# Forgetting attention and a SwiGLU block on one core: the first stage's loads in another order, with memsets that hold the loads of the next batches

## The chip, the cores and the metric

The kernel runs on one core of a Trainium2 chip. The metric is the device time of one execution in microseconds (us), from the start of the program to its end on the chip; the time of a kernel is the median of several executions. The engines are called PE (TensorE, matrix products), ACT (ScalarE), DVE (VectorE), POOL (GpSimd) and SP (SyncE, which here only issues transfers). DMA transfers are issued by SP and ACT into one hardware queue (q1 in the profile) and by POOL into a software queue (q0).

## What is computed

Eight batches of eight heads, 576 tokens, 64 features per head. First a causal attention whose scores carry a decay from a gate f, then a SwiGLU block over all 4608 tokens. Inputs and output are float32.

```python
# q, k, v: (8, 8, 576, 64); f: (8, 8, 576)
scores = q @ k.transpose(0, 1, 3, 2) / sqrt(64)
cum = cumsum(log(clip(f, 1e-4, 1.0)), axis=-1)
scores = where(causal, -1e9, scores + cum[:, :, :, None] - cum[:, :, None, :])
attn = softmax(scores, axis=-1)
x = (attn @ v).transpose(0, 2, 1, 3).reshape(4608, 512)

g, val = x @ w_gate, x @ w_val        # (512 x 1536) each
out = (g * sigmoid(g) * val) @ w_out  # (1536 x 512)
```

## The kernel before

**A plan made at build time.** The class `Plan` (L33) is a list scheduler in Python. Every step of the kernel is an `op` (L52) with an engine or several engines and their costs, the steps that it comes `after`, the buffers that it takes or uses, a priority `key` (the smallest runnable key goes first on its engine), a due time `ready`, and for a transfer its length `dma` and its weight `pkt`. `run` (L76) plays this model forward, and where it starts a step it emits the step's instructions. What reaches the chip is only the order of the instructions on each engine, the choice of buffers, and semaphores for the dependences of data; the due times and costs leave no other mark. In the model, transfers share the DMA between the rings of SP, ACT and POOL in proportion to `pkt` (L111 and L126, with a factor 1.2 where more than one ring is busy), and a transfer counts as landed 1.0 us after its last byte. While the plan has PE idle between 0.6 us and `IDLE_TO` (L904), it emits filler matmuls that nothing reads (`dummy`, L892; `idle=` in L896).

**The work.** A pair is two heads of one batch: 32 pairs, four per batch. For each pair the scores (`score`, L655) are computed transposed, keys on the partitions, from the buffer QK, whose rows hold 64 features and four rows of decay; ACT takes the exponential (`expo`, L663), POOL sets the upper triangle to zero (`mask`, L672), PE multiplies with the values in VB (`weigh`, L686; a column of ones gives the sums), DVE inverts the sums (`invert`, L693) and scales (L700 or L702), PE transposes the result (`flip`, L710), and `put` (L715) writes it to xT. The feed-forward block takes tiles of tokens from xT: twelve groups each of matmuls with wg and wv (`gate`, L787), the activation from tanh on ACT (L791) and two DVE steps (L795, L799), then per 128 tokens twelve matmuls with wo (`project`, L803), a copy (L808) and a store by SP (L811). The first tile is batch 0's 256 first tokens and the second its 320 others, which share their buffers; then come eight tiles of 512 tokens.

**The first stage, batch 0.** q and k are loaded in two halves, a (256 tokens, `ld_a`, L484) and b (320 tokens, `ld_b`, L487), for four heads each, then cast (`cast_1`, L490, through L334 on ACT or L336 on DVE), transposed by PE (L509) and copied to QK (`straighten1`). v goes straight to VB, cast by POOL's transfers (`ld_vc`, L550), in five chunks of 128 tokens (the last of 64). Attention is done for the first half of the tokens of all four pairs and then for the second half.

**The first stage, batch 1** (`FIRST = 2` batches come this way). q and k of a pair are loaded by SP (`ld_qk`, L481), cast on POOL or DVE (`cast_t`, L493), transposed (L498), copied. Its decay rows are four transfers (`row`, L437, in the list `o_row1`) from `dec`, which `blank` (L367 to L371) and `up`, `high`, `rest`, `middle` and `low` (L421 to L434) have filled. v comes as in batch 0. Four buffers BF, into which `cast_t` writes, are blanked by POOL (L363).

**Batches 2 to 7.** POOL casts q and k of a pair into an array `qk_d` in DRAM (`narrow`, L520), SP loads them transposed (`turned`, L529), then the decay rows from `dec_d` (`rows`, L532), which two transfers `dec_out` (L467) wrote earlier. v is loaded by SP into natv (`ld_v`, L539) and cast on POOL (L336). A pair may start these steps at `release(p)` (L478): `PACE0 + (p - 8) * PACE`.

**Weights.** wg, wv and wo come in three chunks each, cast by POOL's transfers (`weights`, L783 and L780).

**What sets the order around the change.** The constants at the end (L900 to L909) are due times and limits of the plan: `W_AT` and `WO_AT` for the chunks of the weights, `Q1_AT` for the pairs of batch 1, `V1_AT` for its v, `DEC_AT` for the decay steps; `FK` is the key of the shared first two tiles of the feed-forward block (`ffn`, L823), `HOLD` holds the first transposes, and `SF` and `TF` end the time in which scores, and transposes of batch 1, may use other PSUM banks. The keys are given in the list at L859 to L890, of which the change touches these:

```python
    for n in range(2):
        values(0, n, -6 + 0.1 * n)
    for n in range(2, NB):
        values(0, n, 2 + 0.1 * n)
```

So two chunks of batch 0's v go first on POOL's queue (key -6), then the first chunks of wg and wv (-5.5), then the other three chunks of v (2).

Of the kernel before, what the change touches and what calls it, by code (L numbers as in the profile page):

```python
# [32 lines left out]
class Plan:  # L33


    PIPE = {"PE": 0.25, "ACT": 0.2, "DVE": 0.2, "POOL": 0.2}

    SPAN, WARM = 3.413, 0.40

# [9 lines left out]
        w = int(t / self.SPAN)  # L49
        self.done_work[w] = self.done_work.get(w, 0.0) + dur * share  # L50

    def op(self, eng, fn, after=(), take=(), use=(), key=0.0, ready=0.0, dma=None, pkt=50.0):  # L52
        o = Op(eng, fn, list(after), list(take), list(use), key, ready, dma)
        o.pkt = pkt
        for b in o.use:
            b.left += 1
        self.ops.append(o)
        return o
# [17 lines left out]
    def run(self, idle=None):  # L76
# [7 lines left out]
        ready = {e: [] for e in engines}  # L84
# [17 lines left out]
        while left:  # L102
# [4 lines left out]
            while events and events[0][0] <= t + 1e-9:  # L107
                _, _, kind, o = heapq.heappop(events)
                if kind in ("queue", "dma"):
                    busy_rings = [r for r in rings.values() if r]  # L110
                    whole = sum(r[0][1].pkt for r in busy_rings) / (1.2 if len(busy_rings) > 1 else 1.0)  # L111
                    for r in busy_rings:
                        r[0][0] -= (t - moved) * r[0][1].pkt / whole
                        while r and r[0][0] < 1e-6:
                            over, n = r.pop(0)
                            if r:
                                r[0][0] += over
                            n.done = t + 1.0
                            push(n.done, "end", n)
                            push(n.done, "done", (n, None, False))  # L120
                    moved = t
                    if kind == "queue":
                        rings[o.ran].append([o.dma, o])
                    busy_rings = [r for r in rings.values() if r]
                    if busy_rings:
                        whole = sum(r[0][1].pkt for r in busy_rings) / (1.2 if len(busy_rings) > 1 else 1.0)  # L126
# [85 lines left out]
PADS = (512, 960, 1344)  # L212
NQK, NPT0, NPT, NVB, NNV, NXN, NTH, NHH, NOT, NRC = 8, 6, 5, 3, 6, 3, 4, 16, 3, 4
FIRST = 2
LEAD = 12.0
PACE, PACE0 = 9.83, 60.3


@with_exitstack
def kernel(ctx, tc, q, k, v, f, w_gate, w_val, w_out, out):  # L220
# [213 lines left out]
        nc.vector.tensor_sub(dec[3][:, 1], r1, dec[2][:, 1])  # L434

    def row(e, r, b, a, z):
        E[e].dma_start(  # L437
            out=QK[D + r : D + r + 1, b * FB : (b + 1) * FB, :, a:z].rearrange("o p x s -> o (p x) s"),
            in_=dec[r][b * H : (b + 1) * H, :, a:z],
        )  # L440
# [19 lines left out]
    m = op(("DVE", dve(n, False)), middle, after=[x], key=k0, tag="middle")  # L460
    x = op(("DVE", dve(n, False)), low, after=[m], key=k0, tag="low")
    gates = [u, g, m, x] + turned_cum
    o_row1 = [op(("SP", SPi), row, r, 1, 0, S, after=gates + o_dec, key=95, dma=0.9, pkt=60.0, tag=("row1", r)) for r in range(4)]
    o_warm = op(("ACT", 1.4), lambda e: nc.scalar.activation(warm, cum[:1, :1], AF.Exp), after=lns + prior, key=-4)

    def dec_out(e, i):
# [75 lines left out]
        m = min(P, S - n * P)  # L542
        copy(e, VB[hvb[b].i][:m, n, :, :D], natv[bv.i][:m])

    v_ready = {}
    LOADK = {0: 0, 1: 300}

    def ld_vc(e, b, n):
# [2 lines left out]

    def values(b, n, key, after=(), ready=0.0):
        if b < FIRST:
            v_ready[b, n] = op(("POOL", 0.9), ld_vc, b, n, after=[v_ready[b, 0]] if n and b else [], key=key, ready=ready, dma=1.5 if n < NB - 1 else 0.8, pkt=25.0,
                               **({"take": [hvb[b]]} if n == 0 else {"use": [hvb[b]]}), tag=("v", n))
            return
        bv = Buf("nv")
        o = op(("SP", SPi), ld_v, b, n, bv, take=[bv], key=key, dma=1.6 if n < NB - 1 else 0.8, pkt=25.0, after=after,
               ready=ready)
        eng = ("POOL", pool(H * D))  # L560
        v_ready[b, n] = op(
            eng, cast_v, b, n, bv, after=[o, o_vb[b % NVB]], use=[bv], key=key,
            **({"take": [hvb[b]]} if n == 0 else {}),
        )
        if n:
            v_ready[b, n].use.append(hvb[b])
            hvb[b].left += 1
            v_ready[b, n].after.append(v_ready[b, 0])
# [5 lines left out]
    def first_queries(g, key_a, key_b):  # L574
        for part, kk0, ld, m, nt, lo in (("a", key_a, ld_a, P, TA, 0), ("b", key_b, ld_b, PB, TB, HALF)):
            n = 4 * nt * D
            casts = []
            for x, nm in enumerate("qk"):
                kk = kk0 + 0.1 * x + 0.2 * g
                bn = Buf("nata") if part == "a" else Buf("natb", "natw")  # L580
                o1 = op(("ACT", 0.55) if part == "a" and x and g else ("SP", SPi), ld, g, nm, bn, take=[bn], key=kk, ready=2.0 if part == "a" and x and g else 0.0,
                        dma=1.06 if part == "a" else 1.2, pkt=33.0 if part == "a" else 60.0, tag=("ld" + part, g, x))
                o2 = op({"DVE": n / 1350 + 0.12, "ACT": act(n)}, cast_1,
                        lambda bn=bn, part=part: nat["nata"][bn.i] if part == "a" else nat[bn.pool][bn.i][:PB], part, x, g, m,
                        after=[o1, o_one[part]], use=[bn], key=kk, tag=("cast" + part, g, x))
# [2 lines left out]
            for h4 in range(4):  # L588
# [5 lines left out]
                first_turned.append(o3)  # L594
                first = p not in took
                o4 = op({"ACT": act(2 * m * nt) + 0.05, "DVE": dve(2 * m * nt)}, straighten1, h, bt, m, nt, lo,
                        after=[o3] + ([took[p]] if not first else []),
                        take=[hqk[p]] if first else [], use=[bt] if first else [bt, hqk[p]], key=kk, tag=("str" + part, h))
# [4 lines left out]
    def queries(p, key, after=(), ready=0.0):  # L603
        done = []
        b = p // FB
        if b < FIRST:
            rest = []
            for x, nm in enumerate("qk"):
                bn, bb, bt = Buf("nat", ("natb", 60.0)), Buf("bf"), Buf("t", ("f", TF), ("s", 22.0))
                kk = key + 2 * x  # L610
                o1 = op(("SP", SPi), ld_qk, p, nm, bn, take=[bn], key=kk, dma=1.2, pkt=100.0, after=after, ready=ready + 0.9 * x,
                        tag=("ldqk", p))
                o2 = op({"POOL": 1.05, "DVE": 0.7}, cast_t,
                        lambda bn=bn: nat[bn.pool if bn.pool == "nat" else "natb1"][bn.i], bb,
                        after=[o1] + o_bf, take=[bb], use=[bn], key=kk, tag=("cast", p))
                o3 = op(("PE", mm(*[P] * QT)), turn, bb, bt, after=[o2, o_id], take=[bt], use=[bb], key=kk, tag=("turn", p))
                for u in range(2):
                    first = not rest
                    rest.append(op(
                        {"ACT": 0.65, "DVE": 0.75}, straighten, p, x, u, bt,  # L620
                        after=[o3] + ([rest[0]] if rest else []),
                        take=[hqk[p]] if first else [], use=[bt] if first else [bt, hqk[p]], key=kk, tag=("str", p),
                    ))
            done = rest
        else:
            ns = [op(("POOL", 0.55), narrow, p, x, key=key + x, ready=release(p) - LEAD, dma=0.9, pkt=60.0, after=after, tag=("narrow", p))
                  for x in range(2)]
            ts = []
            for j in range(2):
# [231 lines left out]
    for n in range(2):  # L861
        values(0, n, -6 + 0.1 * n)
    for n in range(2, NB):
        values(0, n, 2 + 0.1 * n)
    for c in range(NCH):
        for nm, t, src in (("g", wg, w_gate), ("v", wv, w_val)):
            w_ready[nm, c] = op(("POOL", SW), weights, t, src, c, key=-5.5 if not c else 20 + 4 * c, dma=3.0, pkt=95.0,
                                ready=W_AT[c], tag=("w", nm, c))
    for c in range(NCH):
        w_ready["o", c] = op(("POOL", SW), weights, wo, w_out, c, after=wo_free, key=30 + c, dma=3.0, pkt=95.0, ready=WO_AT[c],  # L870
                             tag=("w", "o", c))
    for p in range(FB, FIRST * FB):
        queries(p, 100 + 10 * p, ready=Q1_AT[p - FB])
# [35 lines left out]
TF = 21.3  # L909


# [28 lines left out]
```

## Time and profile before

| what | value |
|---|---|
| runs | 405.73, 406.21, 403.23 us; median 405.73 |
| profiled execution, its time | 407.84 us |
| its span | 406.1 us |
| mean granted clock of PE | 0.976 |
| PE busy | 389.8 us (96%), 3141 matmuls |
| DVE, ACT, POOL busy | 222.8, 219.8, 148.3 us |
| moved by DMA | 50.05 MB; q1 36.25 MB, q0 12.98 MB |
| matmuls L787 (wg, wv), L803 | 111.6 + 111.0, 105.1 us |
| matmuls L655, L686 | 74.8, 44.0 us |

The span is the stretch from the first to the last recorded instruction of the profiled execution, and all starts in the traces count from its beginning. The granted clock is the share of full speed that the throttle gave to PE. Busy times are sums over an engine's instructions; the engines run beside each other, so only what PE, or whatever ends last, waits for is on the path. "L787" is line 787 of the kernel.

### The profile page before, as it was taken

How to read it: one execution, taken by the hardware profiler on the slowest of the kernel's cores; microseconds unless marked ns; L12 is line 12 of the kernel's file. 1: busy time of each engine (PE TensorE's matmuls, PEld its weight loads, DVE VectorE, ACT ScalarE, POOL GpSimd, SP SyncE). 2: the span in 40 equal slices, each digit the busy share in tenths (PEclk: the TensorE clock that was granted, in tenths of full speed). 3: DMA queues.
4: the chain of work that ended last, by engine and by line, in shares of the span. 5: the costliest groups of instructions: out<-in, count | busy, mean ns of one | idle time of the engine just before them, and what ended most of it. 6: DMA issues, size and time to landing. Idle time of an engine off the chain costs nothing.

```text
span 406.1 us, 8530 instructions
## 1 busy us (share of the span) xinstructions
PE 389.8 (96%) x3141; PEld 230.4 (57%) x3186; DVE 222.8 (55%) x440; ACT 219.8 (54%) x451; POOL 148.3 (37%) x380
## 2 busy tenths in 40 slices
PE   7788999989999999999999999999999999999995
PEld 5766977645556655654565555555555544444542
DVE  3556876324773377427742776177616761760850
ACT  3958689534556645653656466556656522323321
POOL 9449387522534353444344344434422100000000
PEclk9859999999999999999999999999999999999998
DMA  9999999487975996489659954886642002002002
GB/s 176 247 150 176 232 187 138 100 158 102 179 133 106 178 209 121 78 164 205 118 123 159 209 113 69 189 194 122 91 136 60 2 0 105 0 2 103 0 22 70
DMA packets 113434, 50.05 MB, mean 123 GB/s; under 512 B 97840, under 2 KB 107760, under 8 KB 112624
## 3 DMA queue, kind: packets, MB, share of 16 engines
q1 hardware_dynamic: 97200, 36.25, 42.7%
q0 software_dynamic: 15664, 12.98, 23.2%
q8 instruction: 25, 0.41, 0.4%
q10 hardware_dynamic: 528, 0.26, 0.2%
q14 instruction: 17, 0.14, 0.1%
HBM read 38.34 MB, written 16.96 MB: 136 GB/s over the span
## 4 chain that ended last, share of the span: by engine, by line
PE 88%; DMA 5%; ACT 2%; SPq 2%; issue 1%; POOL 1%; DVE 1%; ACTq 0%; DVEq 0%
PE ps L787 44%; PE ps L803 23%; PE ps L655 10%; PE ps L686 7%; DMA wo<-in_k_dram 4%; PE ps L710 2%; DMA QK<-dec_d 1%; SPq L487 1%; PE ps L509 1%; ACT PT L663 1%; PE ps L498 1%; ACT QK L334 1%; POOL PT L672 0%; SPq L484 0%; ACT th L791 0%
## 5 line engine op out<-in xcount | busy, mean ns | idle before, releaser
L787 PE MATMUL ps<-xT,wg 128*128 128x512 bf16 (+3 forms) x468 | 111.6, 358 | 0.6
L787 PE MATMUL ps<-xT,wv 128*128 128x512 bf16 (+3 forms) x468 | 111.0, 357 | 0.5
L795 DVE SCALAR_TENSOR_TENSOR th<-th,ps 128x512 f32<-128x512 f32 (+3 forms) x120 | 75.6, 631 | 62.1 <-ACT th L791 62.1
L791 ACT ACTIVATE th<-ps 128x512 f32<-128x512 f32 (+3 forms) x120 | 66.5, 556 | 79.5 <-PE ps L787 77.6
L663 ACT ACTIVATE PT<-ps 128x512 bf16<-128x512 f32 (+2 forms) x192 | 91.9, 507 | 31.3 <-PE ps L655 24.1
L803 PE MATMUL ps<-wo,hh 128*128 128x512 bf16 (+1 forms) x423 | 105.1, 381 | 1.2
L672 POOL TENSOR_SCALAR_AFFINE_SELECT PT<-PT 128x128 bf16<-128x128 bf16 (+1 forms) x192 | 53.4, 281 | 88.9 <-ACT PT L663 81.9
L799 DVE TENSOR_TENSOR hh<-th,ps 128x512 bf16<-128x512 f32 (+3 forms) x120 | 75.9, 634 | 12.4 <-PE ps L787 0.6
L655 PE MATMUL ps<-QK 68*128 68x320 bf16 (+4 forms) x448 | 74.8, 267 | 2.5 <-DMA QK<-dec_d 1.8
L787 PEld LDWEIGHTS <-wv 128*128 128x128 bf16 x480 | 45.3, 97 | 37.3 <-issue 0.7
L787 PEld LDWEIGHTS <-wg 128*128 128x128 bf16 x480 | 45.1, 98 | 37.1 <-issue 0.4
L803 PEld LDWEIGHTS <-hh 128*128 128x128 bf16 (+1 forms) x444 | 41.5, 99 | 38.9 <-issue 1.9
L672 POOL TENSOR_SCALAR_AFFINE_SELECT PTa<-PTa 128x256 bf16<-128x256 bf16 x64 | 26.4, 417 | 74.3 <-ACT PTa L663 72.7
L686 PEld LDWEIGHTS <-PT 128*128 128x128 bf16 x768 | 37.4, 98 | 16.2 <-POOL PT L672 1.4
L655 PEld LDWEIGHTS <-QK 68*128 68x128 bf16 x448 | 37.4, 99 | 15.8 <-DMA QK<-dec_d 1.9
L693 DVE RECIPROCAL rc<-ps 128x5 f32<-128x5 f32 (+2 forms) x64 | 12.3, 192 | 59.7 <-PE ps L686 59.7
L686 PE MATMUL ps<-VB,PT 128*128 128x65 bf16 x768 | 44.0, 194 | 0.4 <-POOL PT L672 0.3
L808 ACT ACTIVATE ot<-ps 128x512 f32<-128x512 f32 (+1 forms) x37 | 22.1, 597 | 37.9 <-PE ps L803 34.7
L663 ACT ACTIVATE PTa<-ps 128x384 bf16<-128x384 f32 x64 | 30.6, 491 | 19.6 <-PE ps L655 19.6
L700 DVE TENSOR_TENSOR xn<-ps,rc 128x320 bf16<-128x320 f32 x56 | 27.5, 492 | 1.9
L336 DVE COPY xT<-ps 128x576 bf16<-128x576 bf16 (+2 forms) x30 | 13.3, 445 | 20.2 <-PE ps L710 19.3
L336 POOL CAST VB<-natv 128x512 bf16<-128x512 f32 (+1 forms) x30 | 18.2, 614 | 7.1 <-DMA natv<-in_v_dram 7.1
(72 smaller groups left out, 203.3 us busy)
## 6 DMA issues: line engine op xcount, KB each, us to landing
out_dram<-ot SPq DMA_DIRECT2D x35, 256.0 KB
natv<-in_v_dram SPq DMA_DIRECT2D x24, 256.0 KB
qk_d<-in_q_dram POOLq DMA_DIRECT2D x24, 144.0 KB, 3.3
qk_d<-in_k_dram POOLq DMA_DIRECT2D x24, 144.0 KB, 4.1
wg<-in_moe_w_gate_dram POOLq DMA_DIRECT2D x3, 512.0 KB, 14.5
wv<-in_moe_w_val_dram POOLq DMA_DIRECT2D x3, 512.0 KB, 18.6
wo<-in_moe_w_out_dram POOLq DMA_DIRECT2D x3, 512.0 KB, 8.6
QK<-qk_d SPq DMA_TRANSPOSE x96
```

Source lines behind the costliest of these rows:

```text
L336: E[e].tensor_copy(dst, src)
L655: nc.tensor.matmul(s[:, c : c + w], QK[:KR, hqk[p].i, 2 * j + 1, kt * P : (kt + 1) * P], QK[:KR, hqk[p].i, 2 * j, q0 : q0 + w], start=True ...
L663: nc.scalar.activation(place(h, i)[:, OFFS[i] : OFFS[i] + c], ps(bs)[:, :c], AF.Exp, scale=0.125)
L672: nc.gpsimd.affine_select(out=d, in_=d, pattern=pat, compare_op=ALU.is_ge, fill=0.0, base=0, channel_multiplier=-1,)
L686: nc.tensor.matmul(o[:, lo : lo + D + 1], pt[:, c : c + P], VB[hvb[b].i][:, kt, hb, : D + 1], start=first and n == 0, stop=last and n == l ...
L700: nc.vector.tensor_mul(XN[bx.i][:, qb : qb + nq, j], o, r)
L787: nc.tensor.matmul(ps(bf)[:, :n], w[:, ko, fc * P : (fc + 1) * P], xT[:, ko, t0 : t0 + n], start=(ko == 0), stop=(ko == KD - 1))
L791: nc.scalar.activation(TH[bt.i][:, :n], ps(bf)[:, :n], AF.Tanh, scale=0.5)
L795: nc.vector.scalar_tensor_tensor(out=t, in0=t, scalar=1.0, in1=ps(bf)[:, :n], op0=ALU.add, op1=ALU.mult)
L799: nc.vector.tensor_mul(HH[bh.i][:, lo : lo + n], TH[bt.i][:, :n], ps(bf)[:, :n])
L803: nc.tensor.matmul(ps(bf)[:m, :DM], HH[hs[fc].i][:, lo : lo + m], wo[:, fc, :], start=(fc == 0), stop=(fc == KF - 1))
L808: nc.scalar.activation(OT[bo.i][:m], ps(bf)[:m, :DM], AF.Copy, scale=0.5)
```

## The change

It alters the plan's model, keys, and due times, and adds one kind of instruction. No arithmetic of the result is changed.

- All five chunks of batch 0's v have key -6, so they stand ahead of the first weights in POOL's queue.
- A new step `mark` memsets one element of the buffer into which a load will go, on DVE. It stands ahead of each of batch 1's eight loads of q and k (`ldqk`) and the five loads of v of batch 2, which come `after` it; it takes the buffer that the load took before, and so SP's load waits on DVE's memset.
- Batch 1's four `row` transfers have key 400 in place of 95, the two `dec_out` transfers 401 in place of 98.
- Two kinds of steps without instructions (`homes`, `v_home`) take the slots of QK and VB for the first two batches at the plan's start.
- The model: SP gets a pipe delay of 0, a transfer may count as landed later (`late`; `LATE` is 2.0), the factor for several rings is `GAIN = 1.12`, and several `dma` and `pkt` are others.
- Due times and constants are others, among them `PACE` 9.24 (9.83), `PACE0` 56.8 (60.3) and `FK` 1200 (2000).

The diff, cut to its core:

```diff
-    PIPE = {"PE": 0.25, "ACT": 0.2, "DVE": 0.2, "POOL": 0.2}
+    PIPE = {"PE": 0.25, "ACT": 0.2, "DVE": 0.2, "POOL": 0.2, "SP": 0.0}
...
-                    whole = sum(r[0][1].pkt for r in busy_rings) / (1.2 if len(busy_rings) > 1 else 1.0)
+                    whole = sum(r[0][1].pkt for r in busy_rings) / (GAIN if len(busy_rings) > 1 else 1.0)
...
-                            push(n.done, "done", (n, None, False))
+                            push(n.done + n.late, "done", (n, None, False))
...
-LEAD = 12.0
-PACE, PACE0 = 9.83, 60.3
+LEAD, LATE = 12.0, 2.0
+PACE, PACE0 = 9.24, 56.8
...
-    o_row1 = [op(("SP", SPi), row, r, 1, 0, S, after=gates + o_dec, key=95, dma=0.9, pkt=60.0, tag=("row1", r)) for r in range(4)]
+    o_row1 = [op(("SP", SPi), row, r, 1, 0, S, after=gates + o_dec, key=400, dma=0.9, pkt=60.0, tag=("row1", r)) for r in range(4)]
...
-    o_decd = [op(("SP", SPi), dec_out, i, after=gates + o_dec, key=98, dma=0.8, pkt=80.0) for i in range(2)]
+    o_decd = [op(("SP", SPi), dec_out, i, after=gates + o_dec, key=401, dma=0.8, pkt=80.0) for i in range(2)]
...
+    homes = [op(("SP", 0.001), lambda e: None, take=[hqk[p]], key=-20) for p in range(FIRST * FB)]
...
+    def mark(e, view):
+        E[e].memset(view()[:1, :1, :1], 0.0)
...
-        o = op(("SP", SPi), ld_v, b, n, bv, take=[bv], key=key, dma=1.6 if n < NB - 1 else 0.8, pkt=25.0, after=after,
-               ready=ready)
+        m = []
+        if b == FIRST:
+            m = [op(("DVE", 0.07), mark, lambda: natv[bv.i], take=[bv], key=-4, ready=ready, tag="mark")]
+        o = op(("SP", SPi), ld_v, b, n, bv, take=[] if m else [bv], use=[bv] if m else [], key=key, dma=1.6 if n < NB - 1 else 0.8, pkt=25.0, late=LATE,
+               after=list(after) + m, ready=ready)
...
-                        dma=1.06 if part == "a" else 1.2, pkt=33.0 if part == "a" else 60.0, tag=("ld" + part, g, x))
+                        dma=1.06 if part == "a" else 1.2, pkt=33.0 if part == "a" else 30.0, late=0.0 if part == "a" else 1.0, tag=("ld" + part, g, x))
...
-                o1 = op(("SP", SPi), ld_qk, p, nm, bn, take=[bn], key=kk, dma=1.2, pkt=100.0, after=after, ready=ready + 0.9 * x,
-                        tag=("ldqk", p))
+                view = lambda bn=bn: nat[bn.pool if bn.pool == "nat" else "natb1"][bn.i]
+                o1 = op(("DVE", 0.07), mark, view, take=[bn], key=-4, ready=ready + 0.9 * x, tag=("mark", p))
+                o1 = op(("SP", SPi), ld_qk, p, nm, bn, use=[bn], key=kk, dma=1.06, pkt=30.0, late=LATE, after=[o1], tag=("ldqk", p))
...
     for n in range(2, NB):
-        values(0, n, 2 + 0.1 * n)
+        values(0, n, -6 + 0.1 * n)
...
-            w_ready[nm, c] = op(("POOL", SW), weights, t, src, c, key=-5.5 if not c else 20 + 4 * c, dma=3.0, pkt=95.0,
+            w_ready[nm, c] = op(("POOL", SW), weights, t, src, c, key=-5.5 if not c else 20 + 4 * c, dma=2.6, pkt=82.0,
...
-W_AT = [0, 9.3, 20.7]
-WO_AT = [23.4, 26.9, 38.7]
-Q1_AT = [28.0, 36.4, 36.5, 46.9]
-V1_AT = 31.9
+W_AT = [0, 2.3, 14.0]
+WO_AT = [34.3, 37.9, 46.1]
+Q1_AT = [21.3, 29.4, 32.2, 33.6]
+V1_AT = 25.0
 IDLE_TO = 28.0
-DEC_AT = 27.1
-FK = 2000.0
+GAIN = 1.12
+DEC_AT = 16.9
+FK = 1200.0
 HOLD = 7.6
-SF = 21.6
-TF = 21.3
+SF = 24.8
+TF = 13.4
```

More of the change, by code (lines that the diff above doesn't have):

```diff
@@ L50, in work, with op @@
         self.done_work[w] = self.done_work.get(w, 0.0) + dur * share
-    def op(self, eng, fn, after=(), take=(), use=(), key=0.0, ready=0.0, dma=None, pkt=50.0):
+    def op(self, eng, fn, after=(), take=(), use=(), key=0.0, ready=0.0, dma=None, pkt=50.0, late=0.0):
         o = Op(eng, fn, list(after), list(take), list(use), key, ready, dma)
-        o.pkt = pkt
+        o.pkt, o.late = pkt, late
         for b in o.use:
@@ L436, in row @@
     def row(e, r, b, a, z):
+        assert all(hqk[b * FB + i].i == b * FB + i for i in range(FB))
         E[e].dma_start(
@@ L553, in values @@
         if b < FIRST:
-            v_ready[b, n] = op(("POOL", 0.9), ld_vc, b, n, after=[v_ready[b, 0]] if n and b else [], key=key, ready=ready, dma=1.5 if n < NB - 1 else 0.8, pkt=25.0,
-                               **({"take": [hvb[b]]} if n == 0 else {"use": [hvb[b]]}), tag=("v", n))
+            if n == 0:
+                v_home[b] = op(("SP", 0.001), lambda e: None, take=[hvb[b]], key=-20, dma=None)
+            v_ready[b, n] = op(("POOL", 0.9), ld_vc, b, n, after=[v_home[b]], use=[hvb[b]], key=key, ready=ready, dma=(1.3 if b else 1.75) if n < NB - 1 else 0.9, pkt=30.0, late=LATE if b else 0.0,
+                               tag=("v", n))
             return
         bv = Buf("nv")
-        o = op(("SP", SPi), ld_v, b, n, bv, take=[bv], key=key, dma=1.6 if n < NB - 1 else 0.8, pkt=25.0, after=after,
-               ready=ready)
+        m = []
[3 more added lines that the diff above has]
+               after=list(after) + m, ready=ready)
         eng = ("POOL", pool(H * D))
@@ L596, in first_queries @@
                 o4 = op({"ACT": act(2 * m * nt) + 0.05, "DVE": dve(2 * m * nt)}, straighten1, h, bt, m, nt, lo,
-                        after=[o3] + ([took[p]] if not first else []),
-                        take=[hqk[p]] if first else [], use=[bt] if first else [bt, hqk[p]], key=kk, tag=("str" + part, h))
+                        after=[o3, homes[p]],
+                        use=[bt, hqk[p]], key=kk, tag=("str" + part, h))
                 if first:
@@ L620, in queries @@
                         {"ACT": 0.65, "DVE": 0.75}, straighten, p, x, u, bt,
-                        after=[o3] + ([rest[0]] if rest else []),
-                        take=[hqk[p]] if first else [], use=[bt] if first else [bt, hqk[p]], key=kk, tag=("str", p),
+                        after=[o3, homes[p]], use=[bt, hqk[p]], key=kk, tag=("str", p),
                     ))
@@ L625, in queries @@
         else:
-            ns = [op(("POOL", 0.55), narrow, p, x, key=key + x, ready=release(p) - LEAD, dma=0.9, pkt=60.0, after=after, tag=("narrow", p))
+            ns = [op(("POOL", 0.55), narrow, p, x, key=key + x, ready=release(p) - LEAD, dma=0.9, pkt=60.0, late=LATE, after=after, tag=("narrow", p))
                   for x in range(2)]
```

8 lines of the change are left out of this document (4 added, 4 removed).

## The prediction

> **What bounds the kernel now.** First the page's 40 slices (10.2 us each): TensorE (PE) has nine or more tenths in almost every slice, and the granted clock (PEclk) falls at the start only, in slices two to four.
>
> ```profile
> PE   7788999989999999999999999999999999999995
> PEclk9859999999999999999999999999999999999998
> ```
>
> So the kernel is PE-bound from about 40 us on, and time can be won only where PE is idle, runs fillers (L894, matmuls with no use, 11.5 us of them, all before 30 us) or has half its clock. Second, the busy time by stretch shows where. Columns: stretch, its length, busy us (instructions) of PE, PEld, DVE, ACT, POOL, then the granted clock, DMA share, GB/s.
>
> ```profile
> 18.21:21.62 3.41, 0.73 (x20) 0.68 (x17) 1.45 (x3) 1.70 (x4) 1.56 (x4) 1.00 1.60 237
> 21.62:25.03 3.41, 2.88 (x26) 2.39 (x26) 2.10 (x9) 1.46 (x4) 0.00 (x0) 0.50 1.77 183
> 25.03:28.45 3.42, 3.42 (x44) 3.16 (x43) 2.64 (x4) 2.29 (x5) 2.19 (x5) 0.50 1.03 174
> 28.45:31.86 3.41, 3.41 (x25) 2.45 (x24) 0.00 (x0) 3.00 (x9) 3.35 (x8) 0.50 0.27 20
> 86.47:89.88 3.41, 1.64 (x22) 0.96 (x21) 0.69 (x2) 0.54 (x1) 0.00 (x0) 1.00 0.89 170
> 89.88:93.30 3.42, 3.42 (x19) 1.55 (x16) 0.40 (x1) 1.07 (x3) 0.69 (x2) 0.50 1.21 136
> ```
>
> Two losses: PE stands still around 20 us and then has half its clock for 10.2 us; and it stands still at 88 us and has half its clock for 3.4 us. In all other stretches from 32 us to the end it is full. Third, the chain of work that ended last names what ends these waits (start, length, what).
>
> ```profile
> 6.04 14.80 DMA wo<-in_k_dram
> 20.86 0.69 DVE natv L336
> 25.84 2.15 PE ps L509 x32
> 28.01 0.70 ACT QK L334
> ...
> 83.02 1.02 SPq L529
> 84.14 0.89 SPq L811
> 85.21 4.39 DMA QK<-dec_d
> 89.64 0.73 PE ps L655 x4
> ```
>
> The last load of batch 0's k lands at 20.8; DVE's cast of it (L336) stands in DVE's order ahead of the first reciprocal (21.47), so PE waits 3.21 us for DVE though the data of the first half is there. At 88 us PE waits for batch 2's decay rows, which SP issued only after a store. Fourth, POOL's own order (start, length, instruction):
>
> ```profile
> 26.79 2.77 POOL L363 MEMSET BF<- 32x768 bf16 x4
> 29.52 0.76 POOL L783 DMA_DIRECT2D wg<-in_moe_w_gate_dram  x1
> 30.27 0.75 POOL L783 DMA_DIRECT2D wv<-in_moe_w_val_dram  x1
> 31.08 0.74 POOL L672 TENSOR_SCALAR_AFFINE_SELECT PT<-PT 128x128 bf16<-128x128 bf16 x3
> ```
>
> 5.0 us of memsets and weight issues without a mask (L672) between 26.8 and 31.1, while PE needs masked tiles for L686.
>
> **The change, part by part.** The order of the changed kernel's instructions is read from its program; durations are from the one profiled execution before (407.84 us, span 406.1; 2.1 above the median 405.73).
>
> *Loads.* v's three later chunks go ahead of the weights on POOL's queue. From 5 to 10 us, with v beside them, SP's queue moved 1341 packets (268 per us); from 11.5 to 17.5, with weights beside them, both queues moved 765, one for one (128 per us). The second half of q and k, 4 x 320 KB in packets of 1 KB, is 1280 packets: 10.0 us at the second rate, 4.8 at the first (of smaller packets, so a bound). I take the middle, 7.4. The first of the four lands at 13.7 either way, so the last lands 3/4 x 2.6 = 2 us earlier, at 18.9 (bounds 17 and 20.8). Weights come later: before, wv's first chunk landed at 4.17+18.6 = 22.8 and the v behind it by 6.65+18.6 = 25.2; the same packets in the other order put wv at 25.2 at most. The first FFN matmul needs it at 28.7 (below), so this costs nothing; if that cover were gone it would be 2.4 us. wg and wv of the third chunk are issued near 19 and 21 instead of 29.5 and 30.3.
>
> *DVE's order.* The reciprocals now stand ahead of the late casts, which removes the 3.21 us wait. What is late next is POOL: the first-half masks ended at 19.8 and now have one weight issue (0.76) among them: 20.5. wv's issue behind (0.75) waits for v's third chunk; before, with two weight chunks ahead, that landed at 24.1, now by about 20: 21.3 (if late, up to 2.8 more).
>
> *POOL from 21.3.* Two masks need ACT's exponentials: ACT is through its first eight at 18.7, then a cast (1.06), two copies (0.38 each), the decay copy (0.67), an exponential, two copies of 0.7, one more: 23.1, so masks until 23.4. The four BF memsets stay (2.77): 26.1. Then up to the last mask of batch 0: 22 masks x 0.25 = 5.5, two VB blanks 1.4, batch 1's v (five issues, 0.90 and 0.71 for the last; before one at 39.1 and four at 57.0) 4.3, two casts 1.64, one wo issue 0.76: 13.6, end 39.7. Before, the last of them ended at 44.6.
>
> *PE.* It stops at head 0's third mask (26.4) and head 1's last (2.4 us of POOL work later, 28.75). The first FFN group (L787) follows at 28.7 against 30.8. From there to batch 0's last L686 the order has 15 groups x 0.436 = 6.5, scores of four heads x 0.53 = 2.1, 72 L686 x 0.0335 = 2.4, two L498 and three L710 groups 1.2, two fillers 0.2: 12.4. The like sum for before, 31.9 to 45.45, gives 11.2 plus 1.24 idle, so the trace takes 9% more than the rows: 13.5, end 42.2. Before, this point is 45.45 with 13 groups done. Gain: 45.45 + 2 x 0.436 - 42.2 = **4.1 us** (5.2 without the 9%).
>
> *22 more fillers* (64 become 86), at 0.12 each 2.6 us of PE. Those before 28 lie inside waits for masks, so I take nothing; the bound is 2.6.
>
> *Memsets as holds.* Thirteen one-element DVE memsets (0.07 each, 0.9) come ahead of batch 1's eight q and k loads and batch 2's five v loads. DVE was busy 10.96 of 13.6 us between 31.9 and 45.5, so nothing for the time itself. Four wait: for a buffer's cast on POOL or a DMA. Behind them in DVE's order stand L795 and L799, and behind these PE. The casts end on POOL at about 35 and 37.7, before DVE comes to these memsets (after the third and seventh gate, 35 and 38.5): nothing, bound 2 us. On SP, the loads block what follows: the decay rows of batch 1 (L437, four), two dec_d stores, then transposes. Before, rows were issued from 35.5 and landed by 44.7; now SP passes the first load when DVE has done three blanks (2.1), at about 25, and the rows go out by 28, needed at 43: nothing. The removal of batch 1's first pair (0.59 MB from 9.6) from the early queue can only help weights; it is inside the bound above.
>
> *Batch 2's start.* Its rows were issued at 85.21 behind the third store and landed 4.39 later, with PE waiting 1.77 and then 3.42 us at half clock (half lost, 1.7). In the new order they go behind the fourth store, but PE's first score of batch 2 has moved behind 12 L803 of 64 rows (2.6) and five FFN groups of 0.86 more. From the fourth output tile to that score: 0.3 + 2.6 + 4.3 = 7.2 us; the chain copy 0.6, store issue 0.9, rows 0.3, landing 4.4 is 6.2. Gain **3.5 us** (bounds 0 and 3.5).
>
> *PACE 9.83 to 9.24.* Pairs are released 0.59 us sooner each. PE is full either way (225.75 of 227.7 us, 93 to 321): nothing, with the rival below.
>
> Sum: 4.1 + 3.5 = 7.6. 407.8 - 7.6 = 400.2 for such a profiled execution, and from the median 405.73: **398.1 us**.
>
> **A rule against the trace.** In the new order PE idles from about 24.8 to 26.4, so the stretch 25.03 to 28.45 is busy for some 2.0 of 3.4 us. The rows: 1.64 busy lost the clock, 2.83 (31.86 to 35.27) kept it; 2.0 is undecided. Once lost, a stretch busy throughout (25.03 to 28.45, 3.42) did not bring it back, one at 89.88 did.
>
> The Trainium skill, TensorE: Matmul & The Clock Gate, Part 1, says that about one busy window of 3.4 us releases the clock. By that rule a lost clock costs one window, 1.7 us, and the sum is 399.8; the trace, with two busy stretches at half clock, disagrees, so I price by rows.
>
> **Rivals.** (1) *The clock falls in the first stage too.* From 21.6 to 31.9 the new order has some 9.2 us of PE work at full clock; at half clock 10.3 us hold 5.1, so 4.1 us are pushed out and the first gain is gone: 405.73 - 3.5 = 402.2. For it: before lost the clock here. Against: the new fillers and no 3.2 us stop. (2) *Batch 2 still waits for its rows* behind the fourth store: 405.73 - 4.1 = 401.6. For it: 1 us of slack only. (3) *The first stage moves nothing*, because DMA sets it anyway (share above 1.0 until 25 us) and batch 2 waits too: about 405. Against: after 21 us the trace's waits are for DVE, ACT and POOL. (4) *Slower: SP cannot feed pairs every 9.24 us.* PE's order is fixed, so if supply stays at 9.83, PE stands 0.59 us in each of 24 pairs, 14.2 us, and FFN work moves to the end: 405.73 - 7.6 + 14.2 = 412.3. It makes the kernel slower once supply takes over 9.24 + 7.6/24 = 9.56 us a pair. Against: from 100 to 320 us SP's transposes waited 24.9 + 17.6 us for PE to free a buffer, 1.8 us a pair of slack.
>
> **How the numbers follow.** Chances: the forecast 0.45, (1) 0.2, (2) 0.13, (3) 0.12, (4) 0.1. A measurement tells about 1%, 4 us, from no change. The forecast's own range is 395.5 (without the 9%, and a little for earlier POOL work) to 400. The range must reach (1), (2) and (3), and leaves out (4) and a tail below: 395.5 to 405.5. Faster by over 1% (below 401.7): the forecast, (2), and a part of (1), 0.65; same: the rest of (1) and (3), 0.24; slower 0.11.
>
> **What would show it.** Right: no PE wait for DVE near 20 us, first FFN matmul near 28.7, last L686 line of batch 0 near 42, no PE wait at 85 to 90 us, PEclk 1.0 there. Wrong: clock 0.5 beyond 25 us (1); a wait for QK<-dec_d in the chain (2); PE idle in front of scores after 95 us (4); POOL's or DVE's waits for SP's loads between 30 and 60 us, for which I have taken nothing.

## The result, and the profile after

The changed kernel takes 401.38 us (median of 14 executions, 399.86 to 403.94), the kernel before 405.31 us (14 executions, 403.23 to 409.76): a ratio of 0.991, 95% interval 0.9885 to 0.9936, so about 3.9 us or 0.9% less. The two profiled executions differ by more: 400.98 us (span 399.2, mean granted clock 0.994) against 407.84, 6.9 us. Why these two differences are not the same is the first question of what follows.

The slices of the changed kernel's page (10 us each): the granted clock dips once, in the third, and PE's dip in the ninth slice (8 before) is gone.

```profile
PE   8879999999999999999999999999999999999995
PEclk9989999999999999999999999999999999999999
```

Busy time by stretch, with the columns of before. First the stretches around 25 us, then those at batch 2's start:

```profile
22.75:26.17 3.42, 1.28 (x14) 0.52 (x12) 3.32 (x7) 2.18 (x5) 3.33 (x7) 1.00 1.24 207
26.17:29.58 3.41, 3.41 (x30) 2.63 (x31) 0.49 (x1) 2.26 (x5) 3.04 (x9) 0.50 1.18 246
29.58:32.99 3.41, 3.41 (x57) 3.11 (x56) 2.56 (x6) 2.24 (x6) 2.52 (x7) 1.00 1.32 218
...
85.00:88.00 3.00, 2.95 (x14) 1.25 (x14) 0.00 (x0) 1.02 (x2) 0.00 (x0) 1.00 0.86 201
88.00:91.00 3.00, 2.99 (x14) 1.18 (x12) 2.35 (x4) 0.77 (x2) 0.00 (x0) 1.00 1.31 222
```

One stretch of 3.4 us has half its clock, where before had three in a row, and from 85 to 91 us PE is full. The rows of batch 2 still come only just in time. They stand in the chain of work that ended last (start, length, what), and PE waits 0.15 us for them:

```profile
87.41 3.60 DMA QK<-dec_d
91.00 0.14 issue
91.14 0.54 PE ps L665 x4
```

What PE waited for in the first 100 us (instruction, what it waited for, us in total, times, longest): of before

```profile
PE ps L686 <- DVE xn L702: 3.2, 1, 3.2
PE ps L509 <- DVE rs L414: 1.8, 1, 1.8
PE ps L655 <- DMA QK<-dec_d: 1.8, 1, 1.8
```

and of the changed kernel (L696 is before's L686, L682 its L672):

```profile
PE ps L696 <- POOL PT L682: 2.1, 1, 2.1
PE ps L904 <- DVE warm L358: 1.3, 1, 1.3
PE ps L696 <- DMA VB<-in_v_dram: 1.2, 1, 1.2
```

The wait for DVE's scaling is gone; PE now waits for one mask of POOL, and at 14 us for v's second chunk, which landed at 15.1 in place of 14.0. What holds the mask stands in POOL's order of the changed kernel:

```profile
21.83 0.24 POOL L682 TENSOR_SCALAR_AFFINE_SELECT PT<-PT 128x64 bf16<-128x64 bf16 x1 [1.26 <-ACT PT L673]
22.13 3.08 POOL L363 MEMSET BF<- 32x768 bf16 x4
25.28 0.75 POOL L682 TENSOR_SCALAR_AFFINE_SELECT PT<-PT 128x128 bf16<-128x128 bf16 x2
```

An account for PE's first 46 us, worked out in the same way for each profiled execution. Idle, fillers, and half of what PE did besides fillers at half clock are losses; the rest of 46 is useful work, so a difference in the last column is time won or lost by then. It is added up from the matmuls' records and the granted clock.

| kernel | idle | fillers | half clock | useful |
|---|---|---|---|---|
| before | 7.8 | 9.7 | 5.8 | 22.7 |
| before, second profile | 8.5 | 10.8 | 5.2 | 21.5 |
| changed | 5.2 | 13.0 | 1.0 | 26.7 |
| v behind the weights | 3.9 | 13.2 | 2.4 | 26.5 |
| DVE's order undone | 5.8 | 13.8 | 1.0 | 25.4 |
| 46 fillers | 4.1 | 7.6 | 6.3 | 28.0 |
| BF on DVE | 3.1 | 12.1 | 0.0 | 30.8 |
| before, DVE's order alone | 5.5 | 9.4 | 3.2 | 27.8 |

The changed kernel is 4.1 us ahead of before at 46 us, and 7.4 at 95 us. Of the second profile of before it is 5.2 us ahead at 46 us and 5.3 at 95, so against that one the whole gain is made in the first stage. One kernel below, with both parts undone, is not in the table: its profiled execution is one of its long ones (411.03 us, median 408.12), so only its waits are read from it.

### The profile page after: what moved, and what is told of

It is laid out like the page before. It is cut to its first block, busy times and chain, and to the rows that moved or that the text cites. A ratio compares the mean times of both kernels' runs of the same rounds, so it can differ in the third digit from the quotient of the medians.

```text
span 399.2 us, 8595 instructions
## 1 busy us (share of the span) xinstructions
PE 387.1 (97%) x3164; PEld 228.7 (57%) x3208; DVE 225.5 (56%) x457; ACT 217.9 (55%) x447; POOL 147.2 (37%) x380
## 3 DMA queue, kind: packets, MB, share of 16 engines
q1 hardware_dynamic: 97200, 36.25, 45.4%
## 4 chain that ended last, share of the span: by engine, by line
PE 85%; DMA 7%; DVE 3%; issue 1%; SPq 1%; ACT 1%; POOL 0%; ACTq 0%; POOLq 0%; DVEq 0%
PE ps L797 43%; PE ps L813 24%; PE ps L665 10%; PE ps L696 6%; DMA VB<-in_v_dram 3%; PE ps L720 2%; DMA dec_d<-xT 2%; DMA xT<-in_k_dram 1%; DVE QK L336 1%; DMA QK<-dec_d 1%; SPq L438 1%; DVE xn L712 0%; PE ps L500 0%; ACT ot L818 0%; POOL VB L555 0%
## 5 line engine op out<-in xcount | busy, mean ns | idle before, releaser
L673 ACT ACTIVATE PT<-ps 128x512 bf16<-128x512 f32 (+2 forms) x192 | 92.9, 508 | 31.0 <-PE ps L665 21.0
L813 PE MATMUL ps<-wo,hh 128*128 128x512 bf16 (+1 forms) x426 | 103.6, 379 | 1.0
L682 POOL TENSOR_SCALAR_AFFINE_SELECT PT<-PT 128x128 bf16<-128x128 bf16 (+1 forms) x192 | 52.3, 275 | 82.3 <-ACT PT L673 76.6
L682 POOL TENSOR_SCALAR_AFFINE_SELECT PTa<-PTa 128x256 bf16<-128x256 bf16 x64 | 26.6, 419 | 66.0 <-ACT PTa L673 64.3
L696 PE MATMUL ps<-VB,PT 128*128 128x65 bf16 x768 | 46.6, 193 | 2.2 <-POOL PT L682 2.1
L696 PEld LDWEIGHTS <-PT 128*128 128x128 bf16 x768 | 38.9, 97 | 16.6 <-POOL PT L682 3.1
L665 PEld LDWEIGHTS <-QK 68*128 68x128 bf16 x448 | 36.4, 98 | 13.9 <-DMA out_dram<-ot 0.6
L673 ACT ACTIVATE PTa<-ps 128x384 bf16<-128x384 f32 x64 | 30.7, 489 | 13.1 <-PE ps L665 12.1
L696 PEld LDWEIGHTS <-PTa 128*128 128x128 bf16 x192 | 13.6, 98 | 9.2
```

Source lines behind the costliest of these rows:

```text
L665: nc.tensor.matmul(s[:, c : c + w], QK[:KR, hqk[p].i, 2 * j + 1, kt * P : (kt + 1) * P], QK[:KR, hqk[p].i, 2 * j, q0 : q0 + w], start=True ...
L673: nc.scalar.activation(place(h, i)[:, OFFS[i] : OFFS[i] + c], ps(bs)[:, :c], AF.Exp, scale=0.125)
L682: nc.gpsimd.affine_select(out=d, in_=d, pattern=pat, compare_op=ALU.is_ge, fill=0.0, base=0, channel_multiplier=-1,)
L696: nc.tensor.matmul(o[:, lo : lo + D + 1], pt[:, c : c + P], VB[hvb[b].i][:, kt, hb, : D + 1], start=first and n == 0, stop=last and n == l ...
L813: nc.tensor.matmul(ps(bf)[:m, :DM], HH[hs[fc].i][:, lo : lo + m], wo[:, fc, :], start=(fc == 0), stop=(fc == KF - 1))
```

## The experiments

**The kernel before again.** Is its profiled execution a typical one?

> The kernel before, unchanged, to see how its executions differ. The profiled execution of before took 407.84 us at a mean clock of 0.976; half of the time at half clock is lost, that is (1 - 0.976) x 406 = 9.7 us, about 2 of them in the idle tail. Theory A (the clock differs between executions): the executions near 405 us and below show a clock of 0.98 or more, that is 1.5 to 3 us less loss, and the time falls by about 4 us for each 0.01 of clock. Theory B (the clock is the same in all, and transfers land at other times): all show 0.975 to 0.978 and the times still spread from 403 to 409.

Measured: 405.12 us, ratio 1.0013 (0.9989 to 1.0037). Both theories fall. The clock does differ between executions, 0.978 to 0.992, but the time does not follow it: one of 402.70 us has 0.978, one of 406.48 has 0.987. The second profiled execution (405.79 us) shows instead what the first had alone, at batch 2's start:

```profile
85.00:88.00 3.00, 3.00 (x32) 1.66 (x30) 1.14 (x3) 0.40 (x1) 1.10 (x3) 1.00 0.91 197
88.00:91.00 3.00, 2.91 (x33) 1.54 (x32) 0.69 (x2) 1.18 (x3) 0.69 (x2) 1.00 1.13 158
91.00:94.40 3.40, 3.35 (x35) 1.89 (x34) 1.14 (x3) 2.46 (x6) 1.23 (x4) 1.00 1.06 157
```

PE is full where the first execution waited 1.77 us and then ran at half clock. Here the first stage ended 1.2 us later (last L686 of batch 0 at 46.6 in place of 45.4), and the decay rows landed at 89.10 in place of 89.59: PE came later, the rows sooner, and there was nothing to wait for.

**Is batch 2's wait in the median?**

```diff
 SP, in the kernel before
+rows (L532) of batch 2's first pair
 store (L811) of tokens 256 to 383
-rows (L532) of batch 2's first pair
```

> The kernel before with the decay rows of batch 2's first pair issued by SP ahead of the third output store in place of behind it; nothing else is changed. In the profiled execution of before PE waited 1.77 us for these rows and then lost 1.7 us at half clock; in a second profiled execution it did not wait. Theory A (the wait is a matter of some executions): the median falls by less than 1.2 us, a ratio of 0.997 to 1.002. Rival B (the wait is there in most executions): the median falls by 2 to 3.4 us, a ratio of 0.9915 to 0.995.

Measured: 403.97 us, ratio 0.9988 (0.9962 to 1.0014). Theory A holds: the rows were issued at 82.71 and landed at 84.75, PE does not wait for them, and the median gains nothing that can be told. The 3.4 us are a matter of some executions.

**DVE's order alone, in the kernel before.** Only the two casts of the second group (heads 4 to 7) move, behind the four reciprocals and scalings.

```diff
 def cast_1(e, src, part, x, g, m, now=False):
+    if part == "b" and g and not now:
+        held.append((e, src, part, x, g, m))
+        return
...
+    while len(scaled1) == 4 and held:   # at the end of scale
+        cast_1(*held.pop(0), True)
```

> The kernel before with one part of the change alone: on DVE the two casts of the second group's second halves stand behind the four first reciprocals and scalings in place of ahead of them; every other order is that of before. Theory A (this order is the first stage's gain): PE's wait of 3.2 to 4.1 us near 19 us goes, the stretches from 21.6 us keep more of their clock, and the time falls by 2.5 to 5 us, a ratio of 0.988 to 0.994. Rival B (the wait only moves on, to POOL's memsets and to the second halves that land at 20.8 to 22 us): the time falls by less than 1.2 us, a ratio of 0.997 to 1.

Measured: 399.56 us, ratio 0.9883 (0.9854 to 0.9912). Theory A: this move alone gives at least as much as the whole change. DVE's order in that run (start, length, instruction):

```profile
18.00 0.18 DVE L698 RECIPROCAL rc<-ps 128x4 f32<-128x4 f32 x1
...
18.63 0.68 DVE L336 CAST natv<-xT 80x1024 bf16<-80x1024 f32 x1
20.16 0.69 DVE L336 CAST natv<-wo 80x1024 bf16<-80x1024 f32 x1 [0.86 <-DMA wo<-in_k_dram]
```

The last cast waits for its data as before (landed at 20.14), but nothing stands behind it that could have gone sooner. Before, the first reciprocal stood behind it and started at 21.47; here the fourth starts at 18.00.

**The same part undone in the changed kernel, with and without the early landing.** In the changed kernel q's last second half is cast by ACT, so the two late casts on DVE are those of k's second halves, one of each group. They go ahead of the first reciprocal:

```diff
 def invert(e, bo, br, n):
+    while late:                     # k's second halves, both groups
+        late.pop(0).fn("DVE")
```

> The changed kernel with one thing undone in the order of DVE: its two late casts of k's second halves (0.70 us each) stand ahead of the first reciprocal again; all else as in the changed kernel. The last of these halves lands at 16.3 to 17.5 us here, so the reciprocals start at 17 to 18.2 in place of 15.9 us. Theory A (the order on DVE is what removes the wait of 3.2 us): PE loses 1 to 2.5 us, and the time is 402.5 to 404 us. Rival B (with the data this early the order is of no account): 401 to 402 us.

Measured: 403.78 us, ratio 0.9999 (0.9965 to 1.0033): theory A, the whole gain is gone. The first reciprocal starts at 17.08 in place of 15.85, since DVE waited 1.68 us for data that landed at 16.27:

```profile
16.30 0.86 DVE L336 CAST natv<-wo 80x1024 bf16<-80x1024 f32 x1 [1.68 <-DMA wo<-in_k_dram]
17.08 0.16 DVE L712 RECIPROCAL rc<-ps 128x4 f32<-128x4 f32 x1
```

The trace shows less of the loss than the ratio does: useful work by 46 us is 1.4 us less than in the changed kernel, where the ratios differ by 0.9%, 3.6 us. Its profiled execution (402.43 us) is 1.35 us shorter than its median; where the rest is lost is not shown.

Then v's last three chunks behind the first weights, with the new order on DVE:

```diff
 def ld_vc(e, b, n, again=False):
+    if b == 0 and n > 1 and not again:
+        held.append(n)              # issued behind wv's first chunk
+        return
```

> The changed kernel with the order of every engine kept, except that POOL issues the last three chunks of batch 0's v behind the first chunks of wg and wv again. Theory A (the queue's order is what lets the second halves of q and k land early): their last landing goes from 16.3 back to 19 to 21 us, v's third chunk from 17.1 to 24 us, PE loses 2 to 4 us in the first stage and the time is 403.5 to 405.5 us. Rival B (the order of the instructions on DVE and PE does it, and landings have slack): no second half is waited for, and the time stays at 401 to 402 us.

Measured: 401.92 us, ratio 0.993 (0.9895 to 0.9965). Rival B: the last half landed at 19.33 in place of 16.27, three microseconds later, and its cast did not move. In that run:

```profile
19.82 0.17 DVE L708 RECIPROCAL rc<-ps 128x4 f32<-128x4 f32 x1
...
20.37 0.70 DVE L336 CAST natv<-wo 80x1024 bf16<-80x1024 f32 x1
```

and in the changed kernel:

```profile
19.88 0.17 DVE L703 RECIPROCAL rc<-ps 128x4 f32<-128x4 f32 x1
...
20.42 0.70 DVE L336 CAST natv<-wo 80x1024 bf16<-80x1024 f32 x1
```

The cast's place in DVE's order sets its time, not the data. Both undone:

> Both undone: DVE's two late casts ahead of the first reciprocal, and v's last three chunks behind the first weights on POOL's queue. The last half lands at 19.3 us here, so the reciprocals start near 20 us. Theory A (either part covers for the other, the order on DVE or the early landing; only without both does PE wait): the wait near 19 us is back with 3 to 4 us, and the time is 404 to 406 us, 2 us or more above the kernel with the order on DVE alone undone. Rival B (the gain of the first stage comes from elsewhere): 401 to 402.5 us.

Measured: 408.12 us, ratio 1.0087 (1.0054 to 1.0119), 0.9% above the run with DVE's order alone undone: theory A, by more than it said, and slower than the kernel before. PE's wait for DVE's scaling is back, as the longest; of its waits:

```profile
PE ps L734 <- DVE xn L726: 4.2, 1, 4.2
PE ps L708 <- POOL PT L694: 2.2, 1, 2.2
```

So the early landing is worth 0.9% behind the old order of DVE and nothing that can be told behind the new one. How much of the 0.9% is lost in the first stage itself is open: later, near 100 us, PE waits another 2.7 us for batch 2's rows in this profile, where the run with DVE's order alone undone waits 0.6. What of the rest of the change makes this kernel slower than before was not tested.

**Without the holding memsets** (the body of `mark` becomes `pass`).

> The changed kernel without its thirteen one-element memsets, so that the loads of batch 1's q and k and of batch 2's v go as soon as SP comes to them and their buffers are free; all other orders kept. Batch 1's first pair (0.59 MB) then goes near 10 us. Theory A (nothing of it is on the path: the second halves land up to 2 us later, before their casts are due at 20.4): 401 to 402 us. Rival B (the held loads keep DMA free for the weights, whose last chunks of wg and wv land at 35.3 and 37.9 us, near their use): these land 1.5 to 3 us later, PE waits for them, and the time is 402.5 to 404.5 us.

Measured: 401.74 us, ratio 0.9947 (0.9909 to 0.9985); the interval overlaps the changed kernel's, and the ratio is 0.4% above. Batch 1's first pair was loaded from 10.35 us; the last second half landed at 16.55 and useful work by 46 us is 26.4 (26.7 with them). The last chunks of wg and wv landed at 35.6 and 38.4, 0.3 and 0.5 us later in place of rival B's 1.5 to 3. Whether the memsets give some tenths of a per cent stays open; the whole gain does not hang on them, since the interval without them stays below 1.

**The pace of before** (`PACE, PACE0 = 9.83, 60.3`).

> The changed kernel with the pace of the pairs as before (9.83 in place of 9.24, first release 60.3 in place of 56.8). The first 80 us of the plan stay alike. Theory A (the pace of 9.24 gives nothing: PE is full either way): 401 to 402 us. Rival B (the earlier release is what brings batch 2's decay rows in time): PE waits at its first scores near 86 us, 1 to 2 us and up to 1.7 more at half clock, and the time is 402.5 to 405 us.

Measured: 399.84 us, ratio 0.9897 (0.985 to 0.9944): theory A, the pace gives nothing. Its profile has 1.7 us of wait for batch 2's rows, the sign of rival B, but they do not show in the median, as in the kernel before.

**Fewer fillers**, with the plan as it was.

```diff
 def dummy(i):
+    sent.append(i)
+    if len(sent) > 46:
+        return
```

> The changed kernel with the same plan, but only the first 46 of its 86 filler matmuls are emitted, those up to about 11 us. They took 5.7 us of PE after that. Theory A (the fillers hold the clock and lie inside waits): without them the stretches from 12.5 and from 19.3 us are too empty, one to three more stretches of 3.4 us run at half clock, and the time is 403 to 406 us. Rival B (fillers stand in the way of ready work, 3.3 us more of them than before): the time falls by 1 to 3 us, to 398.5 to 400.5.

Measured: 400.58 us, ratio 0.9912 (0.9886 to 0.9937), the same as with 86. Both theories hold by half, and cancel: PE has 5.4 us less of fillers and 1.2 us more of useful work by 46 us, since idle time did not grow; but 5.3 us more are lost at half clock, in four stretches in a row.

```profile
16.48:19.90 3.42, 3.02 (x38) 2.66 (x39) 2.94 (x9) 2.27 (x5) 2.48 (x5) 0.50 1.43 193
19.90:23.31 3.41, 3.41 (x42) 2.92 (x40) 2.82 (x8) 3.10 (x7) 2.12 (x4) 0.50 1.24 206
23.31:26.72 3.41, 2.65 (x27) 1.67 (x26) 3.31 (x7) 2.28 (x5) 3.28 (x7) 0.50 1.24 207
26.72:30.13 3.41, 3.41 (x34) 2.53 (x32) 1.06 (x4) 2.33 (x6) 3.20 (x11) 0.50 1.19 257
```

**POOL's memsets out of the way.**

```diff
 o_bf: no instruction on POOL
 def idfull(e):
     nc.vector.tensor_copy(idf, ident[:H, :H])
+    for i in (0, 1):
+        nc.vector.memset(BF[i][QP:], 0.0)
...
     nc.vector.tensor_sub(dec[3][:, 1], r1, dec[2][:, 1])
+    for i in (2, 3):
+        nc.vector.memset(BF[i][QP:], 0.0)
```

> The changed kernel with the order of all else kept, but the four memsets of BF (3.08 us on POOL from 22.1) go to DVE: two at its start, where it idles 2.2 us, and two behind its decay steps, where it idles 3.5 us. Theory A (POOL is late at 23.5 us, and PE's wait of 2.12 us there and the half clock from 26.2, 0.97 us, come from it): both go, and the time is 397.5 to 399.5 us. Rival B (the masks there wait for ACT's exponentials anyway): PE's wait shrinks by less than 0.7 us, and the time stays at 400.5 to 402.

Measured: 398.39 us, ratio 0.9865 (0.9833 to 0.9898): theory A. By 46 us PE has 30.8 us of useful work, 4.1 more than the changed kernel, and no stretch of half clock before its idle tail; the first FFN matmul starts at 24.8 in place of 30.0. Of this 0.8 are given back at batch 2's start, where PE, now earlier, waits for the decay rows again. The two longest waits of that run, with none for a mask:

```profile
PE ps L908 <- DVE warm L360: 1.3, 1, 1.3
PE ps L669 <- DMA QK<-dec_d: 0.9, 1, 0.9
```

**And without its last 15 fillers** (as above, with 71).

> The changed kernel with the BF memsets on DVE as in the run of that, and without its last fillers: only the first 71 are emitted, so the 15 behind 18.2 us (2.1 us of PE) are gone. Theory A (with POOL's memsets out of the way PE has enough work there to keep its clock, 10.75 us of 13.6, and fillers only stand in the way): a fall of 1 to 2 us against that run, a ratio to before of 0.981 to 0.984. Rival B (as without 40 fillers, the clock falls to half and takes back what the fillers gave): the same time as with them or up to 2 us more, a ratio of 0.986 to 0.992.

Measured: 398.61 us, ratio 0.9865 (0.983 to 0.9899): the same time, but not by rival B. The clock held, useful work by 46 us rose to 32.1, and the wait for batch 2's rows rose with it, from 0.9 to 1.8 us.

**And with batch 2's rows behind their own transposes.**

```diff
 def turned(e, p, j, x):
     nc.sync.dma_start_transpose(...)
+    if p == FIRST * FB:
+        put8.append(j)
+        if len(put8) == 4:
+            rows("SP", p)           # and not at its later place
```

> The kernel with BF's memsets on DVE and 71 fillers, and with the decay rows of batch 2's first pair issued by SP right behind that pair's last transpose in place of behind two more stores and three more transposes. In that kernel's profiled execution PE waited 1.81 us at batch 2's first scores. Theory A (the rows are late only by their place in SP's order): the wait goes and the time falls by 1 to 2 us, a ratio to before of 0.981 to 0.984. Rival B (the transposes ahead of the rows land at 84 to 86 us anyway, and the scores wait for those, or the gain of an execution's wait doesn't show in the median): the same time, a ratio of 0.985 to 0.988.

Measured: 398.54 us, ratio 0.9839 (0.9784 to 0.9893). The wait is gone: the rows were issued at 79.98 and landed at 84.29, and from 85 to 95 us PE is idle for 0.11 us. The median is not lower; the profiled execution had lost 1.45 us at 9 us, long before the step that was moved. Six executions from 395.98 to 401.26 cannot tell 1 us, so whether this last step helps stays open. The three kernels with BF on DVE, 398.4 to 398.6, have the lowest medians here, though their intervals overlap that of the kernel before with DVE's order alone.

## Why the prediction was right or wrong

*The point.* 401.38 us lies in the range of 395.5 to 405.5, but 3.3 above the forecast of 398.1 and above the forecast's own range, which ended at 400; the range holds it because it was drawn to reach the rivals. The likeliest outcome, faster by over 1%, was just missed: 0.9%. The step that failed is the last of the sum, where 7.6 us worked out in one execution were taken from the median of three. Between the two profiled executions the sum came out closely: 6.9 us. But its term for batch 2's start, 3.5, does not show in the median of before: of its two profiled executions one has the wait, and with the rows ahead of the store the ratio is 0.9988. Without the term the forecast from the median is 401.6, rival (2)'s number, though not for its reason: the gain is missing because before's median did not hold the wait.

*Batch 2's start.* PE is full there, as forecast, but not with the 1 us of slack: the rows land at 91.00 and PE waits 0.15 us, and QK<-dec_d in the chain is the sign that was named for rival (2). The changed kernel has one profile. In those of the runs that alter one thing in it the wait is 0.3 to 1.7 us, so some of its executions may well wait too.

*DVE's order.* Right, and larger than any other part of the change that was tried alone: moved alone it gives 0.9883, undone alone it takes the gain away.

*Loads.* The last half landed at 16.3, outside the bounds of 17 to 20.8: the middle of two rates was too cautious. As a term it still priced at nothing, since the cast stands at 20.4 in DVE's order. Only with the old order does the landing count, by 0.9%. The two parts of the change cover for each other, so their gains do not add.

*POOL next.* Right: PE stopped for POOL's mask, at 23.5 where 24.8 was forecast, for 2.1 us; the first FFN matmul came at 30.0 (28.7), batch 0's last L686 at 42.6 (42.2). That the four memsets are the cause is shown by moving them. Two errors cancel between these points: PE comes there 1.3 us late, and then needs 12.7 us in place of 13.5. So that 4.1 us were forecast and the account has 4.1 is in part luck; against the second profile of before it has 5.2.

*Fillers.* Taken at nothing, with 2.6 as the bound. The account has 3.3 us more of them than before, and removing 40 sets 5.4 us free. That they cost so much, and that they save about as much in clock (5.3 us), the step missed both.

*The clock.* Taken at nothing. The stretch in which PE stops, 22.75 to 26.17 in the changed kernel, is busy for 1.28 us, not for the 2.0 that was called undecided, and half clock beyond 25 us, the sign named for rival (1), came. It came for one stretch: 1.7 us, as the sum of 399.8 allowed for, of which 1.0 is useful work, in place of that rival's 4.1.

*Memsets as holds, and PACE.* Taken at nothing; for PACE the run bears that out, for the memsets it is open within the interval. Rival (4) did not come: from 95 us on PE loses as little as before.

## What to carry to other kernels

When an engine with a fixed order stands at a load, ask first what could go ahead of it; here moving two casts behind ready work gave 1.2% alone, and without such a move the rest of the change, the new order of the loads in it, gave nothing. Before a wait at some place is put into a sum against a median, look for it in a second execution: a wait that depends on which of two things arrives first is there in one and absent in the next. And a gain in an early stage runs into the next fixed date (here decay rows at 88 us), so follow the freed time to where it is next lost.

## What the runs showed of the hardware

In these traces the clock goes not with PE's busy time but with how many rows of the array its matmuls use. Add up over a stretch of 3.41 us the columns of its matmuls at 2400 per us (the price in the plan, L327), each times its share of 128 rows, and divide by 3.41. A matmul that lies in two stretches counts in each by the part of its time there. In 14 profiled executions, up to 100 us, the 28 stretches that were followed by half clock have shares up to 0.365, and all 352 that were followed by full clock 0.376 or more. Busy time does not part the two sets: stretches busy for as much as 3.41 us were followed by half clock, one busy for 1.68 us by full. Columns alone do not either: up to 0.51 against 0.39 or more. No run changed the rows alone, so this is an order found in the traces and not shown by an experiment. It holds in both directions:

| kernel, stretch from | PE busy | share of columns x rows | clock in it | clock after |
|---|---|---|---|---|
| before, 25.0 | 3.42 | 0.33 | 0.5 | 0.5 |
| before, 28.4 | 3.41 | 0.38 | 0.5 | 1.0 |
| changed, 26.2 | 3.41 | 0.40 | 0.5 | 1.0 |
| 46 fillers, 13.1 | 2.61 | 0.31 | 1.0 | 0.5 |
| 46 fillers, 19.9 | 3.41 | 0.32 | 0.5 | 0.5 |

A stretch at half clock that is nearly full of 68-row scores and 80-row transposes (25.0 and 19.9) did not bring it back, those with more 128-row matmuls (28.4 and 26.2) did. The prediction weighed busy time, which is why it had to call 2.0 us undecided.

The Trainium skill, TensorE: Matmul & The Clock Gate, Part 1, has the clock back after about one busy window of 3.4 us. That fits the stretches from 28.4 and 26.2 and differs from those from 25.0 and 19.9, which were as busy and did not bring it back; the measurement decides, and in it the rows count. The same section says that the windows run free and do not start with the kernel. That agrees: the first stretch of full clock begins between 4.0 and 6.8 us after the span's start in these executions, so each cuts the same work into other stretches. That this is why the mean clock of the kernel before ranges from 0.976 to 0.992 is likely but not shown.

The second thing is the price of a memset. In the run with BF on DVE two of the four stand in DVE's order like this, against 3.08 us for all four on POOL:

```profile
1.78 0.79 DVE L356 MEMSET BF<- 32x384 uint32 x2
```

On DVE the same bytes are written as half as many elements, 0.39 us each, on POOL as 768 bf16 elements in 0.77. That is 1.0 ns an element on both, and a bf16 memset of 576 elements on DVE (L367, 0.54 us) is near it, so the gain lies in the number of elements. The Trainium skill, VectorE: DVE Perf Modes, Zero memsets can be issued as uint32 (trn2), describes that form for the Vector engine, and the trace agrees.
